# Routing of the first token list: its ranks, its tables and its place in the order, and the weights issued beside it

## The chip, the core and the metric

The kernel runs on one core of a Trainium2 chip. The core has TensorE (matrix products, PE in the profile; its weight loads are PEld), VectorE (DVE), ScalarE (ACT), GpSimd (POOL) and SyncE (SP), and 16 DMA engines that serve the queues of SP, ScalarE and GpSimd together. Each engine runs its own instructions in order and waits on semaphores for the others. The metric is device time in microseconds (us); lower is better. One percent of this kernel is about 1.9 us.

## What is computed

First attention over 4 batches of 8 heads, 768 positions and 64 numbers a head: heads 0, 2 and 6 see all earlier positions, the others only the first 4 and the last 64. Its output, 3072 tokens of 512 numbers, then goes through a mixture of 8 experts with early exit:

```python
scores = np.where(mask[None, :, :, :], scale * np.matmul(q, k.transpose(0, 1, 3, 2)), -1000000000.0)
a = np.exp(scores - np.max(scores, axis=-1, keepdims=True))
a = a / (np.sum(a, axis=-1, keepdims=True) + 1e-09)
x = np.matmul(a, v)                       # and the heads laid side by side: (3072, 512)

do_compute = (x @ w_skip) > 0
out = x.copy()
xc = x[do_compute]
logits = xc @ w_gate
e_idx = np.argmax(logits, axis=1)
gate_w = softmax(logits)[np.arange(len(xc)), e_idx]
for e in range(8):
    m = e_idx == e
    y[m] = gate_w[m, None] * (np.maximum(xc[m] @ w1[e], 0.0) @ w2[e])
out[do_compute] = xc + y
```

Each expert has w1 (512 x 1024) and w2 (1024 x 512) in float32, 33.5 MB for all.

## The kernel before

**Two plans.** The kernel writes its instructions from two planned schedules. A `Plan` holds operations with an engine, an assumed duration, dependences and a key; `lay` walks assumed time and on each engine takes, of the operations that are ready, the one with the lowest key. So the order on each engine comes from the keys (table `K`) and the assumed durations; on the chip only that order and the semaphores remain. The first plan is the attention with the first half of the routing, the second one is the experts. `HOLD` and `X3` are assumptions of the second plan: when each engine is free for it, and when the output of batch 3 has landed. In the built program the framework may place instructions of the second plan ahead of the last ones of the first where they do not depend on them.

**Attention.** It runs over 16 pairs of heads, i = 0 to 15, four to a batch. A pair's q, k and v are loaded (SP), cast to float16 (`Cq`, `Ck`, `Cv`, mostly GpSimd), transposed (TensorE) and copied out of PSUM (`Oq` on ScalarE, `Ok` on VectorE, `Kx` and `Vx` on GpSimd; `Vx` is the copy vx<-va). TensorE forms the scores (`E`, tile pst), ScalarE takes the exponential (`X`, tile at), TensorE weighs the values (`PV`, line 950, tile opsa). v carries along its products with the gate and skip weights (tiles vT and vw, `Ov`, `Vw`, `Ow`), so that the weighing also yields the expert logits. VectorE normalizes: `Nr` (recs, line 969), `Nl` (lgh, line 976) and `Nx` (x, line 986; of pair 15 ScalarE does it, line 1009). Behind each batch `Gs` sums the logits (glog, line 1000), and x of the batch goes to the output tensor (`xo`, line 995; batch 3 in two halves, one from SP and one from ScalarE).

**Routing.** The tokens that compute are sorted into 16 slots' tiles t = 0 to 15 of 128 rows, two for each expert. Even tiles are filled from a first list, made of batches 0 to 2 (18 columns of 128 tokens); odd tiles take the overflow of the first list and the second list, batch 3 (6 columns). `steps` writes one list: VectorE finds the expert of each token (mx, sub, eq, m2, m2x, oh, cnt), TensorE ranks the tokens within each expert (`ranks`, lines 1099 to 1111, tile rk), VectorE and GpSimd make of the rank two sets of tables, L and R (tiles tL and tR: 128 x 384 elements an instruction for the first list, six L and three R), and TensorE multiplies them into the slots' row numbers and gate weights (`slots`, line 1225, tile mps). `fin_a` ("idxA": msb, idx, gsl) turns the first list's into the indices of the even tiles, `fin` ("idx") those of the odd ones.

**Experts.** GpSimd fetches each tile's 128 rows out of the output tensor by indirect DMA (`G`, line 1305, tiles xga and xg). Even tiles need idxA and the output of batches 0 to 2; odd ones need idx and all four batches. VectorE casts (line 1354), TensorE transposes, then w1 (line 1395, tile hps), ScalarE's ReLU (line 1406, tile ht), w2 (line 1417, tile yps), VectorE adds to the row (line 1423), and GpSimd scatters the rows back (line 1315).

**Weights.** w1 and w2 of 8 experts are 16 tiles, n = 0 to 15. Each is fetched in two halves by GpSimd (line 445), which cast to float16 on the way: 512 KB land for each half, from 1 MB of float32. `PARTS` lists the halves issued during the attention, each with the operation of GpSimd behind which it stands; 11 of the 32. The rest is issued between the gathers and scatters: in `GORDER` a number is a gather of that tile, -1 the next half. At most 8 of GpSimd's DMAs are in flight.

Of the kernel before, what the change touches and what calls it, by code (L numbers as in the profile page):

```python
# [15 lines left out]
ACT = mybir.ActivationFunctionType  # L16
# [12 lines left out]
E = 8  # L29
# [25 lines left out]
class Plan:  # L55
# [332 lines left out]
def kernel(  # L388
# [14 lines left out]
    nc = tc.nc  # L403
# [10 lines left out]
    Ov = out.rearrange("(b n p) d -> b p n d", b=B, p=P)  # L414
# [4 lines left out]
    if used % 1024:  # L419
# [14 lines left out]
    def wtile(n, pool):
# [62 lines left out]
    with tc.tile_pool(name="qk", bufs=1) as qk_pool, \  # L497
# [20 lines left out]
        op, dma = pl.op, pl.dma  # L518
# [128 lines left out]
        K = dict(r=229.5, rp=254, Cq=-153.5, Ck=-310.5, Cv=-193, W=-501,
                 Tq=-7.5, Tk=-7, Oq=506.5, Ok=-46, OkA=-661.5, Kx=-754.5,
                 Tv=-1.5, Ov=-26, Vw=-110, Ow=-501, Vx=-131, E=7.5, X=-43,
                 PV=17.5, Nr=154, Nl=72.6, Nx=-91.8, Gs=62.65, sl=-166.5,  # L650
                 z=-122, Wc=-90, xa=-254)
# [32 lines left out]
        for o in order:  # L684
            w, n = o[:2]
# [151 lines left out]
        for i in range(NPR):  # L837
            k0 = 10 * i
# [200 lines left out]
        for n, (name, eng) in enumerate((("SP", nc.sync), ("ACT", nc.scalar))):  # L1039
            m = NQB // 2 * n  # L1040
# [20 lines left out]
        def route(ph, c0, n, fns, pool, psum):  # L1061
# [15 lines left out]
            rl = t("rl", [P, n], FP16)  # L1077
            if ph == 0:
# [3 lines left out]
                olo, ohi = t("olo", [P, n, 8], FP16), t("ohi", [P, n, 16], FP16)  # L1082
# [34 lines left out]
            v = nc.vector  # L1117
            u = v if ph else nc.gpsimd

            def rsel_full():  # L1120
                v.tensor_mul(rsel, rk(), o)
                if ph == 0:
# [26 lines left out]
                                                op=ALU.add),  # L1149
# [12 lines left out]
            if ph == 0:  # L1162
# [3 lines left out]
                    op=ALU.is_ge)  # L1166
# [20 lines left out]
            T[ph, "at"] = table  # L1187

            for m in range(0, n, step):
                e = v if ph else nc.gpsimd  # L1190
                a, b = c0 + m, c0 + m + step
                fns["R", m] = lambda m=m, e=e: e.tensor_tensor(
                    table("R", 0)[:, m:m + step].rearrange(
                        "p c (t v) -> p c t v", v=4),
                    oht[:, m:m + step].unsqueeze(3).to_broadcast(
                        [P, step, nt, 4]),
                    va[:, m:m + step].unsqueeze(2).to_broadcast(
                        [P, step, nt, 4]), op=ALU.mult)
                if ph == 0:
                    for m3 in (m, m + 3):  # L1200
                        fns["L", m3] = lambda m=m3: nc.gpsimd.tensor_tensor(
                            table("L", m)[:, m % 9:m % 9 + 3].rearrange(
                                "p c (h l) -> p c h l", l=8),
                            ohi[:, m:m + 3].unsqueeze(3).to_broadcast(
                                [P, 3, 16, 8]),
                            olo[:, m:m + 3].unsqueeze(2).to_broadcast(
                                [P, 3, 16, 8]), op=ALU.mult)
                    continue
                fns["L", m] = lambda m=m, e=e: e.tensor_tensor(
                    table("L", m)[:, m:m + step],  # L1210
                    iota16.unsqueeze(1).to_broadcast([P, step, P]),
                    rl[:, m:m + step].unsqueeze(2).to_broadcast([P, step, P]),
                    op=ALU.is_equal)
# [17 lines left out]
        def steps(ph, c0, n, k0, last, pool, psum):  # L1231
            f = {}
            route(ph, c0, n, f, pool, psum)
            prev = [last, ("route", 3)]
            w = n * 0.008
            order = ["mx", "sub", "eq", "m2", "m2x", "oh"]
            for nm in order:
                op(("r", ph, nm), "DVE", 0.18 + w, f[nm], prev, k0)
                prev = [("r", ph, nm)]
            op(("r", ph, "ex"), "ACT", 0.25 + w, f["ex"], [("r", ph, "sub")],  # L1240
               -50 if ph else k0 - 30)
            op(("r", ph, "ranks"), "PE", 0.1 * n, f["ranks"],
               [("r", ph, "oh"), ("r", 0, "sums")],
               k0 - 33 if ph == 0 else -50,
               take=None if ph else ("tps", ("r", ph, "rsel")))
            prev = [("r", ph, "oh")]
            on_pool = ("te", "g16", "glo", "rl", "ohi")
            for nm in ["sums", "te", "sm", "gate", "g16", "glo"]:
                op(("r", ph, nm), "POOL" if ph == 0 and nm in on_pool else "DVE",
                   0.17 + w, f[nm],  # L1250
                   prev + ([("r", ph, "ex")] if nm == "sm" else []), k0 + 0.1)
                prev = [("r", ph, nm)]
            prev = [("r", ph, "ranks")]
            if ph:
                op(("r", 1, "oht"), "DVE", 0.2, f["oht"], [("r", 1, "te")],
                   k0 + 0.15)
            for nm in (["rsel", "rank", "rl"] if ph else
                       ["rsel", "rank", "h128", "rl", "tt", "oht", "ge", "hi",
                        "lo", "olo", "ohi"]):
                op(("r", ph, nm), "POOL" if ph == 0 and nm in on_pool else "DVE",  # L1260
                   0.18 + w, f[nm],
                   prev + ([("r", ph, "te")] if nm == "tt" else []),
                   k0 + 0.2)
                prev = [("r", ph, nm)]
            on, ms = ("DVE", [0]) if ph else ("POOL", [0, 6, 12])
            for m in range(0, 1 if ph else n, 3):
                op(("r", ph, "L", m), on, 0.9 if ph else 0.8, f["L", m],
                   [("r", ph, "rl" if ph else "ohi")], K["rp"] if ph == 0 else k0 + 0.3)
            for m in ms:
                op(("r", ph, "R", m), on, 0.6 if ph else 0.9, f["R", m],  # L1270
                   [("r", ph, "oht"), ("r", ph, "glo")],
                   K["rp"] if ph == 0 else k0 + 0.25)
# [57 lines left out]
    with tc.tile_pool(name="moe_w", bufs=1, reuse_waits="tile") as mw_pool, \  # L1330
# [16 lines left out]
        op, dma = pl.op, pl.dma  # L1347
# [148 lines left out]
        for m, t in enumerate(live):  # L1496
            n = of[t][0]
# [6 lines left out]
        for n, (e, ts) in enumerate(jobs):  # L1504
# [94 lines left out]
```

## Time and profile before

| | |
|---|---|
| time, median of 3 runs | 187.7 us (187.51 to 188.92) |
| the profiled execution: its own time / its span | 188.18 us / 186.4 us |
| granted TensorE clock, mean | 0.941 |
| busy share: TensorE / weight loads / VectorE / ScalarE / GpSimd | 79% / 63% / 58% / 55% / 72% |
| chain that ended last, by engine | DMA 51%, PE 14%, POOL 12%, issue 8% |
| DMA time by queue: GpSimd / SP / ScalarE | 54.3% / 38.8% / 2.0% of 16 engines' span |

Times within the profile are counted from the start of the span. The attention ends at about 97 us and the experts follow. The prediction is made against this one execution, which took half a microsecond more than the median. Its page gives this row for the mean share of the DMA engines, in 40 slices of 4.66 us (a digit is a tenth):

```profile
DMA  5999989999999899999999999999999999999520
```

After the load of the first inputs it falls below nine tenths in two slices only, until the last weights are in.

### The profile page before, as it was taken

Reading aid. Unit: us, or ns where it says so; the run is one execution under the profiler, and the core shown is the slowest. Engines: PE = TensorE matmul, PEld = TensorE weight load, DVE = VectorE, ACT = ScalarE, POOL = GpSimd, SP = SyncE. Lnnn points to the kernel's source line nnn. Section 1 sums busy time; section 2 is a strip of 40 time slices with the busy share of each in tenths; the row PEclk is TensorE's granted clock in tenths of the full one; section 3 lists DMA queues with packets and bytes.
Section 4 is the critical chain, followed back from the end, with each engine's and each line's share of the span. In section 5 each row is a group of like instructions: output and inputs, shape, how many; then the busy total and the mean of one; then the engine's idle time right before and its main releaser. Section 6 shows DMA issues by size and latency. Waiting matters only on the chain.

```text
span 186.4 us, 4870 instructions
## 1 busy us (share of the span) xinstructions
PE 148.0 (79%) x1929; PEld 118.3 (63%) x1929; DVE 108.1 (58%) x241; ACT 103.2 (55%) x145; POOL 133.4 (72%) x233
## 2 busy tenths in 40 slices
PE   0689798799999889989933029997997999999900
PEld 0567686698888778878722028876786785757400
DVE  6675567677878748888969523353444355730320
ACT  2575987698998999989629902404203412403000
POOL 7558779999999999997695686356567768525440
PEclk9999999999999999999985558999999999999995
DMA  5999989999999899999999999999999999999520
GB/s 162 315 289 357 342 287 392 390 286 343 276 380 327 274 367 212 203 168 243 252 252 247 353 215 236 213 261 226 262 237 226 183 229 214 200 237 232 148 75 5
DMA packets 27633, 47.12 MB, mean 253 GB/s; under 512 B 5187, under 2 KB 19139, under 8 KB 27603
## 3 DMA queue, kind: packets, MB, share of 16 engines
q0 software_dynamic: 7312, 21.55, 54.3%
q1 hardware_dynamic: 18560, 23.99, 38.8%
q10 hardware_dynamic: 1730, 1.20, 2.0%
q8 instruction: 17, 0.28, 0.6%
q14 instruction: 14, 0.11, 0.2%
HBM read 56.64 MB, written 10.49 MB: 360 GB/s over the span
## 4 chain that ended last, share of the span: by engine, by line
DMA 51%; PE 14%; POOL 12%; issue 8%; SPq 5%; DVE 3%; ACT 2%; POOLq 0%; DVEq 0%
DMA out_dram<-x 13%; DMA w<-in_moe_w_dram 12%; DMA qf<-in_q_dram 9%; DMA xga<-out_dram,idx 7%; DMA out_dram<-xga,idx 6%; DMA xg<-out_dram,idx 5%; PE pst L898 4%; SPq L660 4%; PE opsa L950 3%; PE pst L886 3%; POOL out_dram L1315 3%; PE tps L740 2%; POOL k L712 2%; POOL va L718 1%; POOL q L712 1%
## 5 line engine op out<-in xcount | busy, mean ns | idle before, releaser
L908 ACT ACTIVATE at<-pst 128x1024 f16<-128x1024 f32 (+1 forms) x60 | 58.9, 1013 | 9.7 <-PE pst L898 9.3
L1406 ACT ACTIVATE ht<-hps 128x512 f16<-128x512 f32 x32 | 16.9, 601 | 48.3 <-PE hps L1395 44.2
L898 PE MATMUL pst<-qT,k 128*128 128x128 f16 (+2 forms) x308 | 36.3, 236 | 0.0
L1395 PEld LDWEIGHTS <-w 128*128 128x128 f16 x352 | 31.6, 146 | 4.1 <-issue 1.7
L1395 PE MATMUL hps<-xT,w 128*128 128x128 f16 (+1 forms) x352 | 32.5, 252 | 1.7 <-DVE xT L1379 1.5
L780 DVE COPY k<-tps 64x768 f16<-64x768 f16 x27 | 25.7, 953 | 12.0 <-PE tps L740 11.1
L898 PEld LDWEIGHTS <-k 128*128 128x128 f16 x308 | 24.6, 99 | 10.0 <-issue 3.2
L1417 PE MATMUL yps<-w,ht 128*128 128x512 f16 x128 | 30.4, 379 | 0.0
L886 PE MATMUL pst<-smask,identb 128*128 128x512 bf16 (+2 forms) x64 | 21.6, 348 | 2.3 <-ACT at L908 2.2
L950 PE MATMUL opsa<-va,at 128*128 128x74 f16 x392 | 20.3, 197 | 2.3 <-DVE x L986 2.3
L950 PEld LDWEIGHTS <-at 128*128 128x128 f16 x472 | 18.5, 97 | 2.7 <-DVE x L986 2.5
L445 POOL DMA_DIRECT2D w<-in_moe_w_dram x33 | 18.9, 580 | 1.1 <-PE yps L1417 0.7
L1417 PEld LDWEIGHTS <-ht 128*128 128x128 f16 x128 | 12.0, 98 | 12.1 <-issue 0.5
L1305 POOL DMA_INDIRECT xg<-out_dram,idx x10 | 11.3, 1135 | 9.9 <-ACT ht L1406 4.5
L1315 POOL DMA_INDIRECT out_dram<-xg,idx x10 | 10.1, 1005 | 11.4 <-DMA w<-in_moe_w_dram 4.6
L718 POOL CAST va<-vf 128x768 f16<-128x768 f32 x16 | 13.1, 824 | 1.7 <-DMA vf<-in_v_dram 1.0
L986 DVE TENSOR_TENSOR x<-opsa,recs 128x768 f32<-128x768 f32 x15 | 14.2, 945 | 0.0
L1423 DVE SCALAR_TENSOR_TENSOR xg<-yps,gsl,xg 128x512 f32<-128x512 f32 x10 | 7.4, 747 | 11.4 <-PE yps L1417 11.1
L740 PE MATMUL tps<-ident,q 128*128 128x128 f16 x96 | 8.6, 230 | 6.5 <-DVE q L712 5.9
L766 ACT COPY qT<-tps 128x768 f16<-128x768 f16 x16 | 12.8, 800 | 1.0 <-PE tps L740 0.9
L712 POOL CAST k<-kf 128x768 f16<-128x768 f32 x15 | 12.3, 821 | 1.4 <-PE pst L898 0.8
L1354 DVE CAST x<-xg 128x512 f16<-128x512 f32 x10 | 6.0, 634 | 12.5 <-DMA xg<-out_dram,idx 12.5
(146 smaller groups left out, 252.8 us busy)
## 6 DMA issues: line engine op xcount, KB each, us to landing
w<-in_moe_w_dram POOLq DMA_DIRECT2D x31, 512.0 KB
qf<-in_q_dram SPq DMA_DIRECT2D x16, 384.0 KB, 6.9
kf<-in_k_dram SPq DMA_DIRECT2D x15, 384.0 KB, 6.5
out_dram<-x SPq DMA_DIRECT2D x3, 1536.0 KB, 18.0
out_dram<-x SPq DMA_DIRECT2D x1, 768.0 KB
out_dram<-x ACTq DMA_DIRECT2D x1, 768.0 KB, 8.4
w<-in_moe_w_dram POOLq DMA_DIRECT2D x2, 256.0 KB
kf<-in_k_dram ACTq DMA_DIRECT2D x1, 384.0 KB, 4.5
```

Of the source, the lines that this page charges most:

```text
L445: nc.gpsimd.dma_start(out=wts[e, half][:, c], in_=(w1r, w2r)[half][e][:, c])
L712: e.tensor_copy(t, f)
L718: nc.gpsimd.tensor_copy(vab[i % 3][:, :, GX:GX + 2 * D].rearrange("p n (h d) -> p h n d", h=2), fp32_of("v", i))
L780: nc.vector.tensor_copy(to, ti)
L886: nc.tensor.matmul(pst[:, c0 - c * CH:c0 - c * CH + m].rearrange("p (n c) -> p n c", c=P), identb, mv, start=(n == 0), stop=(n == last))
L898: nc.tensor.matmul(pst[:, c0 - c * CH:c0 - c * CH + m * P], lt, qTs[i][:, qb * P:(qb + m) * P], start=(n == 0), stop=(n == last))
L908: nc.scalar.activation(ats[i][:, c * CH:c * CH + cn], psts[i, c][:, :cn], ACT.Exp, scale=SCALE)
L950: nc.tensor.matmul(opss[i][:, hi, qb * VA:(qb + 1) * VA], ats[i][:, b0 + c:b0 + c + P], vb, start=(n == 0), stop=(n == len(todo) - 1))
L1315: moved(nc.gpsimd.indirect_dma_start(out=out[:n, :], out_offset=bass.IndirectOffsetOnAxis(ap=idx[:, t:t + 1], axis=0), in_=row(t), in_offs ...
L1395: nc.tensor.matmul(hpss[n, b][:, fi, :], w1[:, s, m * b + fi], xTs[n][:, s, :w], start=(fi == 0 and s == 0), stop=(fi == m - 1 and s == DS ...
L1406: nc.scalar.activation(hts[n][:, m * b:m * (b + 1), :w], hpss[n, b], ACT.Relu)
L1417: nc.tensor.matmul(ypss[t], hts[n][:, j, c:c + P], w2[:, j], start=(j == 0), stop=(j == FS - 1))
```

## The change

It edits numbers that set the order, and moves four instructions to another engine. The arithmetic is the same.

- **Ranks.** The first list's `ranks` has a key of its own, `rk` = -44 (before: r - 33 = 196.5), and an assumed duration half as long. A low key lets it stand on TensorE as soon as it is ready.
- **Tables.** Two of the first list's three R (columns 6 and 12) and two of its six L (12 and 15) go from GpSimd to VectorE.
- **The list's keys.** `r`, the key of VectorE's steps of the first list, goes from 229.5 to 93, and the other keys are set anew.
- **Weights.** `PARTS` has 10 halves, not 11: four behind Vx of pair 10 as before, four behind Vx of pair 13 and two behind that of pair 14. Before, four stood behind Cv of pair 14, two behind Vx 13 and one behind Vx 14.
- **The experts' order.** `GORDER` issues gathers 0, 2 and 4 in a row and then three halves; before, a half stood behind each. `HOLD` and `X3` get smaller.

```diff
-    PARTS = [("Vx", 10)] * 4 + [("Cv", 14)] * 4
-    PARTS += [("Vx", 13)] * 2 + [("Vx", 14)]
+    PARTS = [("Vx", 10)] * 4 + [("Vx", 13)] * 4 + [("Vx", 14)] * 2
...
-    GORDER = (0, -1, 2, -1, 4, -1, -1, 1, -1, 3, -1, 5, -1, -1, 6, 7, -1, -1, 8, 9,
+    TAB_DVE = dict(L=(12, 15), R=(6, 12))
+    GORDER = (0, 2, 4, -1, -1, -1, 1, -1, 3, -1, 5, -1, -1, 6, 7, -1, -1, 8, 9,
               -1, -1, 10, 11, -1, -1, 12, 13, -1, -1, 14, 15)
-    HOLD, X3 = dict(POOL=4.5, PE=0.5, DVE=1.0, ACT=4.0), 13.0
+    HOLD, X3 = dict(POOL=0.3, PE=0.0, DVE=0.2, ACT=2.2), 7.5
...
-        K = dict(r=229.5, rp=254, Cq=-153.5, Ck=-310.5, Cv=-193, W=-501,
...
+        K = dict(r=93, rp=245.5, Cq=-155, Ck=-251.5, Cv=-254.5, W=-522,
...
+                 Wc=-90, xa=-254, rk=-44)
...
-                e = v if ph else nc.gpsimd
+                e = v if ph or m in TAB_DVE["R"] else nc.gpsimd
...
-                        fns["L", m3] = lambda m=m3: nc.gpsimd.tensor_tensor(
+                        e3 = v if m3 in TAB_DVE["L"] else nc.gpsimd
+                        fns["L", m3] = lambda m=m3, e=e3: e.tensor_tensor(
...
-            op(("r", ph, "ranks"), "PE", 0.1 * n, f["ranks"],
+            op(("r", ph, "ranks"), "PE", 0.05 * n, f["ranks"],
                [("r", ph, "oh"), ("r", 0, "sums")],
-               k0 - 33 if ph == 0 else -50,
+               K["rk"] if ph == 0 else -50,
...
+                dve = ph or m in TAB_DVE["L"]
+                op(("r", ph, "L", m), "DVE" if dve else "POOL",
+                   0.9 if ph else 0.55 if dve else 0.8, f["L", m],
+                   [("r", ph, "rl" if ph else "ohi")], k0 + 0.3 if dve else K["rp"])
```

What stands where in the built program is seen at three places. The first is GpSimd while pairs 13 and 14 are prepared (w_1_67 and w_1_68 are w1 and w2 of expert 1; vx_143<-va_140 is the copy `Vx` of pair 13). Rows with - stand only before, with + only after:

```order
-L718 CAST va_141<-vf 128x2x6x64
-L787 COPY kx_1_138<-k_1_134 64x4x64
-L788 COPY kx_1_138<-k_1_134 64x4x4
-L445 DMA w_1_67<-in_moe_w_dram 128x2048 x2
-L445 DMA w_1_68<-in_moe_w_dram 128x2048
+L787 COPY kx_1_138<-k_1_134 64x4x64
+L788 COPY kx_1_138<-k_1_134 64x4x4
+L718 CAST va_141<-vf 128x2x6x64
 L823 COPY vx_143<-va_140 64x296
 L825 COPY vx_143<-va_140 64x296
-L445 DMA w_1_68<-in_moe_w_dram 128x2048
```

The three halves ahead of the copy and the one behind it are gone from here; the four follow behind it in two pairs, and one of three halves of expert 2 stands behind the third gather.

The second is TensorE where the first list's product stands (mps<-tR,tL; its first matmul is mps<-c). Before:

```order
L1101 LDWEIGHTS ones_81
L1101 MATMUL rk<-oh,ones_81 128x8
L1106 LDWEIGHTS ones_81
L1106 MATMUL rk<-full,ones_81 128x48
L1222 LDWEIGHTS ones_81
L1222 MATMUL mps<-c_82,ones_81 128x64
L1225 LDWEIGHTS tL_0_2213
L1225 MATMUL mps<-tR_0_2190,tL_0_2213 128x64
```

After, where at is the exponential of pair 14 in the first rows and of pair 15 in the last:

```order
L950 LDWEIGHTS at
L950 MATMUL opsa<-vx_142,at 128x74
L1223 LDWEIGHTS ones_81
L1223 MATMUL mps<-c_82,ones_81 128x64
L1226 LDWEIGHTS tL_0_2209
L1226 MATMUL mps<-tR_0_2178,tL_0_2209 128x64
...
L1226 LDWEIGHTS tL_1_2212
L1226 MATMUL mps<-tR_0_2178,tL_1_2212 128x64
L950 LDWEIGHTS at
L950 MATMUL opsa<-va_139,at 128x74
```

The product stood behind the second list's ranks (rk), which need the logits of batch 3. Now its 19 matmuls stand between the weighing of pair 14 and that of pair 15.

The third is VectorE behind the second list's count (cnt), where msb, idx and gsl are idxA. Before:

```order
L1091 TENSOR_REDUCE cnt<-oh 128x8
L1139 TENSOR_SCALAR r_te<-r_m2x 128x6
L1154 TENSOR_TENSOR r_oht<-iota_86,r_te 128x48
L1121 TENSOR_TENSOR r_rsel<-rk,oh 128x48
L1148 TENSOR_REDUCE r_rank<-r_rsel 128x6
L1158 TENSOR_SCALAR r_rl<-r_rank 128x6
L1209 TENSOR_TENSOR tL_0_2352<-iota_86,r_rl 128x768
L1142 TENSOR_REDUCE r_sm<-r_ex 128x6
L1143 RECIPROCAL r_gate<-r_sm 128x6
L1144 CAST val<-r_gate 128x6
L1145 TENSOR_TENSOR val<-r_gate,val 128x6
L1436 COPY msb<-mps 128x64
```

After:

```order
L1137 SCALAR_TENSOR_TENSOR oh<-r_m2x,r_eq 128x48
L1091 TENSOR_REDUCE cnt<-oh 128x8
L1441 COPY msb<-mps 128x64
L1444 SCALAR_TENSOR_TENSOR idx<-msb 128x8
L1446 TENSOR_TENSOR gsl<-msb 128x8
L1444 SCALAR_TENSOR_TENSOR idx_100<-msb 128x8
L1446 TENSOR_TENSOR gsl_101<-msb 128x8
L1139 TENSOR_SCALAR r_te<-r_m2x 128x6
L1142 TENSOR_REDUCE r_sm<-r_ex 128x6
L1143 RECIPROCAL r_gate<-r_sm 128x6
L1144 CAST val<-r_gate 128x6
```

idxA stood behind ten steps of the second list and now stands right behind cnt. The four tables stand, on VectorE, behind r_olo and ahead of recs, lgh and x of pair 14. On this engine r_rsel, the step that takes up the ranks, now stands ahead of recs, lgh and x of pair 13, and r_olo is behind them as before.

More of the change, by code (lines that the diff above doesn't have):

```diff
@@ L644 @@
         op("mism", "DVE", 1.0, c_mism, ["wgl"], 61)
-        K = dict(r=229.5, rp=254, Cq=-153.5, Ck=-310.5, Cv=-193, W=-501,
[L648 to L651, printed above, removed]
+        K = dict(r=93, rp=245.5, Cq=-155, Ck=-251.5, Cv=-254.5, W=-522,
+                 Tq=-4.5, Tk=-1.5, Oq=564, Ok=-101, OkA=-572, Kx=-820.5, Tv=0,
+                 Ov=-59.5, Vw=-92.5, Ow=-498.5, Vx=-126, E=8.5, X=-90.5, PV=19,
+                 Nr=-5, Nl=64.6, Nx=-218.3, Gs=15.15, sl=-166.5, z=-152.5,
+                 Wc=-90, xa=-254, rk=-44)
         f32 = {}
@@ L1264, in steps @@
                 prev = [("r", ph, nm)]
-            on, ms = ("DVE", [0]) if ph else ("POOL", [0, 6, 12])
+            ms = [0] if ph else [0, 6, 12]
             for m in range(0, 1 if ph else n, 3):
-                op(("r", ph, "L", m), on, 0.9 if ph else 0.8, f["L", m],
-                   [("r", ph, "rl" if ph else "ohi")], K["rp"] if ph == 0 else k0 + 0.3)
+                dve = ph or m in TAB_DVE["L"]
+                op(("r", ph, "L", m), "DVE" if dve else "POOL",
+                   0.9 if ph else 0.55 if dve else 0.8, f["L", m],
+                   [("r", ph, "rl" if ph else "ohi")], k0 + 0.3 if dve else K["rp"])
             for m in ms:
-                op(("r", ph, "R", m), on, 0.6 if ph else 0.9, f["R", m],
+                dve = ph or m in TAB_DVE["R"]
+                op(("r", ph, "R", m), "DVE" if dve else "POOL",
+                   0.6 if ph else 0.55 if dve else 0.9, f["R", m],
                    [("r", ph, "oht"), ("r", ph, "glo")],
-                   K["rp"] if ph == 0 else k0 + 0.25)
+                   k0 + 0.25 if dve else K["rp"])
             if ph:
```

## The prediction, made before the changed kernel had run

> **What bounds the kernel now.** First I read the table by windows. Its columns are the window, its length, the busy time of TensorE, its weight loads, VectorE, ScalarE and GpSimd (number of instructions), the granted TensorE clock, the mean busy share of the 16 DMA engines, and GB/s written.
>
> ```profile
> 72.00:76.00 4.00, 4.00 (x72) 3.49 (x69) 2.70 (x6) 3.69 (x5) 3.75 (x8) 1.00 1.06 217
> 80.00:84.00 4.00, 3.45 (x65) 2.92 (x63) 3.30 (x10) 3.44 (x5) 3.86 (x10) 1.00 0.94 176
> 96.00:100.00 4.00, 0.86 (x20) 0.69 (x16) 2.86 (x8) 2.40 (x13) 4.00 (x6) 0.53 1.07 254
> 100.00:104.00 4.00, 1.41 (x26) 1.26 (x26) 3.66 (x19) 3.64 (x9) 0.19 (x1) 0.50 1.04 296
> 104.00:108.00 4.00, 0.34 (x6) 0.23 (x6) 1.06 (x7) 3.49 (x7) 3.45 (x4) 0.50 1.00 299
> 136.00:140.00 4.00, 4.00 (x34) 3.47 (x32) 1.16 (x3) 0.59 (x2) 2.69 (x4) 1.00 0.95 238
> 168.00:172.00 4.00, 3.77 (x30) 2.90 (x29) 0.00 (x0) 1.29 (x3) 2.51 (x3) 1.00 1.07 230
> 104.00:172.00 68.00, 58.99 (x530) 44.84 (x531) 27.86 (x61) 19.66 (x38) 43.65 (x50) 0.93 1.04 231
> ```
>
> TensorE is almost empty from 93 to 111, but the DMA engines are not: their share is 0.94 or more in every row, even across that hole. The whole second half moves weights. Next the chain of waits and the end of TensorE's timeline (start, duration, what ran, idle time ahead and its cause).
>
> ```profile
> 79.13 23.68 DMA out_dram<-x
> 104.06 0.98 POOL xga L1305
> 158.38 14.23 DMA w<-in_moe_w_dram
> 169.96 1.97 PE L1395 MATMUL hps<-xT,w 128*128 128x256 f16 x16 [0.23 <-DMA w<-in_moe_w_dram]
> 171.76 5.48 PE L1417 MATMUL yps<-w,ht 128*128 128x512 f16 x24
> ```
>
> The last expert's second half of w1, issued at 158.38, is waited for at 169.96; behind it TensorE runs through to the end. So the end is set by when the weight stream reaches that half, and the stream has hardly a pause from 79 on. What counts is how much weight is left behind the first gather, and any pause put into the DMA queue.
>
> **The change, part by part.** (1) One half fewer ahead of the gathers. These are GpSimd's weight issues, the table work and the first gather, and two lines of the page on issue sizes and times to landing.
>
> ```profile
> 78.38 1.58 POOL L445 DMA_DIRECT2D w<-in_moe_w_dram  x3
> 79.94 0.47 POOL L823 COPY vx<-va 64x296 f16<-64x296 f16 x1
> 80.82 0.53 POOL L445 DMA_DIRECT2D w<-in_moe_w_dram  x1
> 82.54 1.05 POOL L445 DMA_DIRECT2D w<-in_moe_w_dram  x2
> 86.47 0.53 POOL L445 DMA_DIRECT2D w<-in_moe_w_dram  x1
> 91.88 1.99 POOL L1192 TENSOR_TENSOR tR<-r_oht,val 128x384 f16<-128x384 f16 x2 [0.48 <-DVE r_oht L1154]
> 94.63 4.77 POOL L1201 TENSOR_TENSOR tL<-r_ohi,r_olo 128x384 f16<-128x384 f16 x6
> 104.04 1.24 POOL L1305 DMA_INDIRECT xga<-out_dram,idx  x1 [3.85 <-DVE gsl L1441]
> 105.28 0.60 POOL L445 DMA_DIRECT2D w<-in_moe_w_dram  x1
> w<-in_moe_w_dram POOLq DMA_DIRECT2D x31, 512.0 KB
> out_dram<-x ACTq DMA_DIRECT2D x1, 768.0 KB, 8.4
> ```
>
> Before, seven halves are issued between 78.38 and 87.0; after, six, in pairs behind the vx copies of pairs 13 and 14, so from about 80.3. In 72:76 only weights move: 512 KB at 217 GB/s is 2.4 us. That half now stands behind the gathers: **+2.4 us** of stream.
>
> (2) The pause that opens. x of batch 2 (1.57 MB, 4.3 us at the 367 GB/s that the next row shows while x of batch 1 goes out) is issued at about 79 with no weights queued.
>
> ```profile
> 64.00:68.00 4.00, 3.63 (x68) 3.14 (x67) 3.08 (x6) 4.00 (x7) 3.81 (x10) 1.00 1.01 367
> ```
>
> It lands well ahead of today's 102.8 (79.13 + 23.68). But the backlog behind 79 shrinks from 7 x 2.4 + 4.3 = 21.1 us to 6 x 2.4 + 4.3 = 18.7 us and starts at about 81 (two us after x's issue, an estimate), so the queue runs dry at 100 to 101. What feeds it next is x of batch 3, then the gathers. When do they come? VectorE and TensorE decide:
>
> ```profile
> 81.23 0.39 DVE L1131 SCALAR_TENSOR_TENSOR r_eq<-r_sub,erev 128x144 f32<-128x144 f32 x1
> 82.33 0.17 DVE L1135 SCALAR_TENSOR_TENSOR r_m2x<-glog,r_m 128x18 f32<-128x18 f32 x1
> 84.24 0.27 DVE L812 CAST va<-vw 128x108 f16<-128x108 f32 x1 [0.80 <-PE vw L805]
> 93.15 0.88 DVE L1174 TENSOR_TENSOR r_olo<-iota,r_lo 128x144 f16<-128x144 f16 x1
> 94.40 0.94 DVE L986 TENSOR_TENSOR x<-opsa,recs 128x768 f32<-128x768 f32 x1
> 98.71 0.75 DVE L1131 SCALAR_TENSOR_TENSOR r_eq<-r_sub,erev 128x48 f32<-128x48 f32 x1
> 99.73 0.47 DVE L1135 SCALAR_TENSOR_TENSOR r_m2x<-glog,r_m 128x6 f32<-128x6 f32 x1
> 100.48 0.25 DVE L1091 TENSOR_REDUCE cnt<-oh 128x8 f16<-128x48 f16 x1
> 101.70 0.96 DVE L1209 TENSOR_TENSOR tL<-iota,r_rl 128x768 f16<-128x768 f16 x1
> 103.33 0.22 DVE L1436 COPY msb<-mps 128x64 f32<-128x64 f32 x1
> 103.92 0.35 DVE L1192 TENSOR_TENSOR tR<-r_oht,val 128x192 f16<-128x192 f16 x1
> 95.40 1.03 PE L950 MATMUL opsa<-va,at 128*128 128x74 f16 x25 [2.34 <-DVE x L986]
> 97.60 2.56 ACT L1009 ACTIVATE x<-opsa,recs 128x64 f32<-128x64 f32 x12 [3.48 <-DVE lgh L976]
> 100.19 0.42 ACTq L995 DMA_DIRECT2D out_dram<-x  x1
> ```
>
> Up to r_olo the change only permutes VectorE's work; its one wait there is the 0.80 at 84.24, and r_olo's 0.88 is long because GpSimd's table ran beside it. With both saved r_olo ends at about 93.0 instead of 94.0. Ranking at once is thus worth at most a microsecond: the ranks came late, but VectorE was full in the meantime.
>
> Then four tables are new on VectorE. Between the 192-element row (0.35) and the 768-element row (0.96), 384 elements take 0.55. Lower bound of four: 2.2 us. Upper bound: each also waits out one GpSimd table (4.77 / 6 = 0.8): 5.4 us. Nearest are r_eq and r_m2x: 0.39 and 0.17 alone, 0.75 and 0.47 beside GpSimd's tables, so 0.3 to 0.36 of waiting each. I take 0.9 a table, 3.6 us: 93.0 to 96.6. GpSimd's four remaining L end at 96.3. Recs, lgh and x of pair 14 follow on VectorE (1.4 us): 98.0. The slots' product now stands ahead of the last pair's weighing on TensorE; it is ready at about 97.2 and so just hidden behind that x; if the tables were later, it would hold the last pair itself. The last pair starts at 98.0 instead of 95.40: +2.6 (bounds: +1.4, +4.5).
>
> That shift carries over to ScalarE's x of batch 3 and its two issues: 102.2 and 102.8 instead of 99.6 and 100.19, so data from about 104.2. Before, the stream passed from x of batch 2 to x of batch 3 at about 101.9 without a pause (1.07 and 1.04 in 96:104). The stream behind it starts **2.3 us later** (+1.1 to +4.2).
>
> (3) The first gather. idxA moves directly behind cnt; that chain also loses 0.7 us of waiting beside tables (r_eq, r_m2x). cnt ends at 100.73 + 2.6 - 0.7 = 102.6 and the gather follows 0.7 later: 103.4 instead of 104.04 (bounds 102.2 and 105.2). What the earlier list gains, the later last pair takes back.
>
> (4) GORDER. Three gathers (1.05 each and 0.3 between) now stand ahead of the first weight issue: 107.4 instead of 105.28. That costs nothing while x of batch 3 (4.3 us) and three gathers fill the engines to about 110; without that cover it would cost up to 2. Gather 1 then waits for x of batch 3, which landed 8.4 us after its issue before: 111.2, with GpSimd there at 109.2 and all later issues queued behind. Three halves (7.2 us) cover that.
>
> (5) The other keys permute the attention of batches 0 to 2: the same instructions, and TensorE and ScalarE stay full in 72:84. I take 0, within 0.5 either way.
>
> (6) Given back: the stream has small pauses today (0.95 in 136:140, 0.94 in 80:84). A longer backlog closes some: 0 to 1.2 us, taken as **-0.6**.
>
> Sum: 2.4 + 2.3 - 0.6 = +4.1 us (ends +2.3 and +6.6). On the profiled execution that is 186.4 + 4.1 = 190.5 us of span (its own time 188.18, half a microsecond over the median); on the median 187.7 + 4.1 = **191.8 us**.
>
> **A rule against the change.** The rows of r_eq and r_m2x show VectorE waiting when both its inputs are in SBUF. The Trainium skill, page "SBUF — State Buffer", section "Who interferes with whom", says that such an instruction and a GpSimd one that reads SBUF exclude each other for the whole instruction. The trace agrees for VectorE; GpSimd's own six tables show no loss (0.8 each). By that rule the eight tables run one after the other.
>
> **Rivals.** Strict turns: 4 x 0.55 + 4 x 0.8 = 5.4 us of tables, last pair at 99.9, gather at 105.2; the upper ends of (2) and (6) make +6, 193.7 us. For it: r_eq, r_m2x and r_olo; against: GpSimd's undisturbed 4.77.
>
> No change: the wait at 169.96 is only 0.23, and TensorE is busy 59 of 68 us from 104 to 172, so it is nearly a bound too. If the pause is the smallest (+1.1), all of 1.2 is recovered, and x and weights that no longer alternate save another us, the delay is about +1: 188.7 us. Against: a stream with share 1.04 has little left to recover.
>
> Faster: the list is what TensorE waits for at 111, and TensorE is the bound behind it. With the gather at 102.2, TensorE starts 1.8 us earlier and the end follows: 185.9 us. It decides if the awaited half lands by 168; today it lands at 169.9 with one half less in front, which speaks against it. That the change does not do what it says is partly so: weights still start a microsecond behind x of batch 2; but the gather waits for idxA, not for that x.
>
> **How the numbers follow.** Forecast 0.47, strict turns 0.18, no change 0.22, faster 0.13. About 1% (1.9 us) is what a measurement of this kernel can tell from no change: slower 0.65, within 0.22, faster 0.13. The range 188.0 to 193.8 leaves out the faster case, the lowest part of no change and the top of strict turns, some 0.2.
>
> **What would show it.** Right: last pair's weighing between 97 and 100; a dip of the DMA share between 99 and 106; first gather within a us or so of 104; x of batch 2 landed before 99; the last weights landing 3 to 5 us later, with longer waits for weights near the end. Wrong: no dip, or the last TensorE block not later though the stream is; or attention ending over a microsecond earlier, which I have priced at nothing.

## The result and the profile after

| | before | changed |
|---|---|---|
| first comparison: median of 4 runs each (range) | 187.6 us (187.44 to 188.92) | 193.34 us (192.08 to 193.87) |
| second comparison (`a_again` below) | 187.38 us (186.27 to 190.28, 7 runs) | 192.46 us (191.54 to 192.94, 4 runs) |
| ratio to before, with its 95% interval | | 1.0305 [1.0248, 1.0361]; 1.0278 [1.022, 1.0335] |
| span of the profiled execution | 186.4 us | 192.2 us |

The changed kernel is slower by 5.7 us (5.1 in the second comparison), 3%; forecast were 4.1 us and a range of 188.0 to 193.8. Medians and ranges here hold every run, ratios leave out the disturbed ones, and where the two disagree it is the ratio that counts.

The table by windows, first two rows of the kernel before that the readings below rest on:

```profile
100.00:112.00 12.00, 3.30 (x46) 2.90 (x47) 5.76 (x26) 7.13 (x15) 7.23 (x10) 0.50 1.03 275
160.00:176.00 16.00, 15.32 (x97) 9.32 (x95) 5.07 (x8) 4.13 (x8) 8.00 (x9) 1.00 0.96 210
```

and of the kernel after:

```profile
96.00:100.00 4.00, 1.37 (x19) 0.93 (x18) 3.97 (x6) 0.00 (x0) 3.48 (x4) 0.72 1.07 215
100.00:104.00 4.00, 2.31 (x36) 2.08 (x34) 1.61 (x6) 0.95 (x5) 0.00 (x0) 0.50 0.35 71
104.00:108.00 4.00, 0.38 (x7) 0.26 (x6) 3.62 (x22) 3.64 (x13) 1.79 (x2) 0.50 0.53 208
160.00:176.00 16.00, 12.34 (x84) 8.10 (x81) 5.46 (x9) 2.06 (x4) 6.80 (x10) 1.00 1.06 234
```

The share of the DMA engines is the number before the last. Where before had 1.04 and 1.00, from 100 to 108, there are 0.35 and 0.53: 4.6 us of DMA time are missing (4 x 0.69 + 4 x 0.47). And near the end, where TensorE was busy for 15.3 of 16 us before, it is busy for 12.3. Its timeline there:

```profile
173.79 1.97 PE L1400 MATMUL hps<-xT,w 128*128 128x256 f16 x16 [0.53 <-DMA w<-in_moe_w_dram]
176.84 1.97 PE L1400 MATMUL hps<-xT,w 128*128 128x256 f16 x16 [1.09 <-DMA w<-in_moe_w_dram]
179.42 3.61 PE L1422 MATMUL yps<-w,ht 128*128 128x512 f16 x16 [0.61 <-DMA w<-in_moe_w_dram]
```

Each of the last blocks now waits for weights, where before had a single wait of 0.23. In the trace, the last packet of weights ends at 175.06 before and at 181.47 after, and the span ends 11.3 and 10.7 later. The time went into the hole behind 100 us. How it came about, by the timelines of VectorE, GpSimd, TensorE, SP and ScalarE, after:

```profile
94.29 0.72 DVE L1174 TENSOR_TENSOR r_olo<-iota,r_lo 128x144 f16<-128x144 f16 x1
94.94 1.65 DVE L1192 TENSOR_TENSOR tR<-r_oht,val 128x384 f16<-128x384 f16 x2
96.51 2.28 DVE L1202 TENSOR_TENSOR tL<-r_ohi,r_olo 128x384 f16<-128x384 f16 x2
99.16 0.94 DVE L986 TENSOR_TENSOR x<-opsa,recs 128x768 f32<-128x768 f32 x1
95.16 4.32 POOL L1202 TENSOR_TENSOR tL<-r_ohi,r_olo 128x384 f16<-128x384 f16 x4 [0.31 <-DVE r_olo L1174]
105.91 1.13 POOL L1310 DMA_INDIRECT xga<-out_dram,idx  x1 [6.43 <-DVE idx L1444]
109.83 1.71 POOL L445 DMA_DIRECT2D w<-in_moe_w_dram  x3
99.54 0.66 PE L1226 MATMUL mps<-tR,tL 128*128 128x64 f16 x9 [0.76 <-POOL tL L1202]
100.16 1.72 PE L950 MATMUL opsa<-va,at 128*128 128x74 f16 x25
113.26 1.86 PE L1400 MATMUL hps<-xT,w 128*128 128x128 f16 x16 [0.58 <-DVE xT L1384]
105.03 0.38 SPq L995 DMA_DIRECT2D out_dram<-x  x1
105.65 0.42 ACTq L995 DMA_DIRECT2D out_dram<-x  x1
```

The tables occupy VectorE until 98.8, so x of pair 14 ends at 100.10; the list's product has its last table at 99.5 and ends at 100.2. Both hold the last pair's weighing, which starts at 100.16 instead of 95.40 and, at a granted clock of 0.50, takes 1.72 instead of 1.03. x of batch 3 is issued at 105.03 instead of 99.58. The ten halves had landed by then (at about 102.6), x of batch 2 too (at 89.4, before at 102.8), so nothing was in the queues. A second execution of the changed kernel (`a_again`) shows the same a microsecond earlier: last pair at 99.01, x of batch 3 issued at 103.88, last weights at 180.55.

### The profile page after: what moved, and what is told of

The parts are those of the page before. It is cut to its first block, busy times and chain, and to the rows that moved or that the text cites. A ratio compares the mean times of both kernels' runs of the same rounds, so it can differ in the third digit from the quotient of the medians.

```text
span 192.2 us, 4852 instructions
## 1 busy us (share of the span) xinstructions
PE 151.4 (79%) x1917; PEld 121.8 (63%) x1929; DVE 109.8 (57%) x245; ACT 103.4 (54%) x145; POOL 131.9 (69%) x229
## 4 chain that ended last, share of the span: by engine, by line
DMA 35%; PE 30%; issue 11%; POOL 7%; DVE 7%; ACT 7%; POOLq 0%; SPq 0%; ACTq 0%; DVEq 0%
DMA w<-in_moe_w_dram 18%; PE pst L898 12%; DMA xg<-out_dram,idx 11%; PE pst L886 5%; PE opsa L950 5%; PE tps L740 4%; ACT at L908 4%; POOL out_dram L1320 3%; DMA vf<-in_v_dram 3%; DMA xga<-out_dram,idx 3%; DVE k L780 3%; PE tps L751 2%; POOL tL L1202 2%; ACT k L778 1%; ACT qT L766 1%
## 5 line engine op out<-in xcount | busy, mean ns | idle before, releaser
L898 PE MATMUL pst<-qT,k 128*128 128x128 f16 (+2 forms) x308 | 37.0, 241 | 0.7 <-ACT at L908 0.7
L1400 PE MATMUL hps<-xT,w 128*128 128x128 f16 (+1 forms) x352 | 33.5, 256 | 3.2 <-DMA w<-in_moe_w_dram 2.6
L1400 PEld LDWEIGHTS <-w 128*128 128x128 f16 x352 | 32.1, 148 | 5.9 <-DMA w<-in_moe_w_dram 3.8
L780 DVE COPY k<-tps 64x768 f16<-64x768 f16 x27 | 25.8, 954 | 12.2 <-PE tps L740 11.3
L898 PEld LDWEIGHTS <-k 128*128 128x128 f16 x308 | 25.2, 101 | 10.4 <-issue 3.8
L950 PE MATMUL opsa<-va,at 128*128 128x74 f16 x392 | 21.2, 201 | 0.0
L950 PEld LDWEIGHTS <-at 128*128 128x128 f16 x472 | 19.4, 101 | 0.2
L886 PE MATMUL pst<-smask,identb 128*128 128x512 bf16 (+3 forms) x52 | 17.8, 354 | 1.6 <-ACT at L908 1.6
L1310 POOL DMA_INDIRECT xga<-out_dram,idx x6 | 7.0, 1174 | 9.4 <-DVE idx L1444 6.4
```

What stands on the lines that cost most here:

```text
L780: nc.vector.tensor_copy(to, ti)
L886: nc.tensor.matmul(pst[:, c0 - c * CH:c0 - c * CH + m].rearrange("p (n c) -> p n c", c=P), identb, mv, start=(n == 0), stop=(n == last))
L898: nc.tensor.matmul(pst[:, c0 - c * CH:c0 - c * CH + m * P], lt, qTs[i][:, qb * P:(qb + m) * P], start=(n == 0), stop=(n == last))
L950: nc.tensor.matmul(opss[i][:, hi, qb * VA:(qb + 1) * VA], ats[i][:, b0 + c:b0 + c + P], vb, start=(n == 0), stop=(n == len(todo) - 1))
L1310: moved(nc.gpsimd.indirect_dma_start(out=row(t), out_offset=None, in_=out[:n, :], in_offset=bass.IndirectOffsetOnAxis(ap=idx[:, t:t + 1], ...
L1400: nc.tensor.matmul(hpss[n, b][:, fi, :], w1[:, s, m * b + fi], xTs[n][:, s, :w], start=(fi == 0 and s == 0), stop=(fi == m - 1 and s == DS ...
```

## The experiments

Each kernel is the changed one (names with a_) or the one before (b_) with the edit shown. The DMA share is that of the window from 100 to 112, where before has 1.03 and the changed kernel 0.63 (0.65 in the second comparison); a share less by 0.1 is 1.2 us of DMA time.

| kernel | median us (runs) | ratio to before [95%] | span | share 100 to 112 |
|---|---|---|---|---|
| `a_half11` | 189.64 (10) | 1.006 [1.0008, 1.0111] | 188.1 | 0.92 |
| `a_half12` | 187.59 (10) | 0.9995 [0.9943, 1.0046] | 185.4 | 1.02 |
| `b_half10` | 190.0 (10) | 1.0055 [0.9997, 1.0113] | 188.0 | 0.82 |
| `b_tab` | 191.88 (4; 189.37 to 193.97) | none | 188.9 | 0.79 |
| `a_again` | 192.46 (4) | 1.0278 [1.022, 1.0335] | 191.2 | 0.65 |
| `a_pool` | 193.35 (4) | 1.0327 [1.0267, 1.0387] | 192.7 | 0.51 |
| `a_late` | 193.62 (4) | 1.0335 [1.0271, 1.04] | 193.1 | 0.46 |
| `a_late_pool` | 190.84 (4) | 1.0228 [1.0166, 1.0289] | 188.3 | 0.78 |
| `a_late_pool_g` | 188.54 (10) | 0.9997 [0.9944, 1.0049] | 186.9 | 0.90 |
| `b_keys` | 186.14 (4) | 0.9883 [0.9807, 0.9959] | 184.8 | 1.06 |
| `a_idx12` | 191.86 (4) | 1.0197 [1.0114, 1.0281] | 189.9 | 1.05 |
| `a_alldve` | 191.69 (1) | none | 190.0 | 0.68 |

The first four were run beside 25 runs of before (median 187.61), the next four beside 7 (187.38), the last four beside 13 (188.28).

### One or two halves more: `a_half11`, `a_half12`

```diff
-    PARTS = [("Vx", 10)] * 4 + [("Vx", 13)] * 4 + [("Vx", 14)] * 2
+    PARTS = [("Vx", 10)] * 4 + [("Vx", 13)] * 4 + [("Vx", 14)] * 3   # * 4 in a_half12
```

The added halves have no duration in the plan, so the order of the attention stays.

> The changed kernel with one more weight half issued behind Vx of pair 14 (11 instead of 10), nothing else moved ahead of the experts. Theory: the 5.7 us lost are DMA time, and most of it is the hole from 101.2 to 106.0 in which the DMA engines have nothing to do; one half is 2.4 us of work that then stands in the hole. So the hole shrinks to about 2.4 us and the time falls by 2.4 us to about 190.9. Rival, TensorE starts its experts late (first product of w1 at 113.26 instead of 111.06) and that sets the end: the time stays at 193.3 within 0.7.

> The changed kernel with two more halves issued behind Vx of pair 14 (12 instead of 10). Theory: the hole of 4.8 us is filled by 2 x 2.4 us, and the time falls by 4.3 to 4.8 us, to 188.5 to 189.0, a microsecond or so above before, which is what the stream lost ahead of 100 us. If TensorE's start, which is still 2.2 us late, shows once the stream is mended, it comes out near 190. Rival, TensorE's start sets the end already: 193.3 within 0.7.

The windows of `a_half12`, and its first product of w1:

```profile
100.00:112.00 12.00, 1.73 (x29) 1.39 (x28) 6.43 (x29) 9.54 (x26) 5.03 (x6) 0.50 1.02 285
```

```profile
113.04 1.86 PE L1400 MATMUL hps<-xT,w 128*128 128x128 f16 x16 [0.58 <-DVE xT L1384]
```

With two halves the hole is gone, and so is the loss: 1.0278 to 0.9995, 2.8% or 5.3 us, though TensorE starts its experts at 113.04, as late as in the changed kernel. TensorE's start is not what it lost by. The 5.3 us are a little more than the 4.3 to 4.8 that were expected. With one half the ratio falls by 2.2%, 4.1 us (by the medians 2.8), more than the 2.4 that were said; part of that is not the half's, since the last pair began at 98.30 there, 0.7 us earlier than in `a_again`. The rival (no gain) falls with both.

### One half fewer, in the kernel before: `b_half10`

```diff
-    PARTS += [("Vx", 13)] * 2 + [("Vx", 14)]
+    PARTS += [("Vx", 13)] * 2
```

> The kernel before with one half fewer (the one behind Vx of pair 14 left to the experts, 10 in all), nothing else moved ahead of the experts. Theory: the weights run out 2.4 us earlier, near 100, x of batch 3 comes no earlier than before, at about 102, so a hole of 2 to 2.4 us opens and the time grows by as much: 189.6 to 190.0. Rival, a half behind the gathers costs nothing since TensorE is the bound from 111 on: 187.6 within 0.7.

The ratio grew by 0.55% (1.0 us, interval 0 to 2.1), the span of the profiled execution by 1.6. The share from 100 to 112 fell from 1.03 to 0.82, 2.5 us of DMA time: the hole is as large as said. By the ratio it cost half of the 2 to 2.4 us that were said; closer than its interval that can't be told.

### The four tables alone, in the kernel before: `b_tab`

```diff
+    TAB_DVE = dict(L=(12, 15), R=(6, 12))
...
-                e = v if ph else nc.gpsimd
+                e = v if ph or m in TAB_DVE["R"] else nc.gpsimd
```

and likewise for L. On VectorE the four stand behind r_olo, on GpSimd they are missing; no other row of the order differs.

> The kernel before with the same four tables of the first list on VectorE behind r_olo, nothing else moved. Theory: in the changed kernel the four took 3.9 us there (94.94 to 98.8), two of them 1.18 us each beside a table of GpSimd; so the last pair's weighing starts at about 99.2 instead of 95.4, x of batch 3 is issued 3.8 us later, a hole of some 3.5 us opens behind 102, and the time grows by 3 to 3.8 us to about 191. Rival, the tables are hidden beside the weight stream: 187.6 within 0.7, with the hole under 1 us.

The last pair's weighing on TensorE:

```profile
99.47 1.72 PE L951 MATMUL opsa<-va,at 128*128 128x74 f16 x25 [5.96 <-DVE x L987]
```

It started at 99.47, after a wait of 5.96 for x of pair 14, where before had 95.40 after 2.34. The share fell to 0.79 (2.9 us). The four executions scatter from 189.37 to 193.97, too widely for a ratio; in the profiled one the last weights land 2.6 us later than before (177.70 against 175.06) and the span is 2.5 us longer, somewhat less than the 3 to 3.8 that were said. Four tables on VectorE are enough to open a hole, and they are not hidden beside the stream.

### What holds the last pair: `a_again`, `a_pool`, `a_late`, `a_late_pool`

```diff
-    TAB_DVE = dict(L=(12, 15), R=(6, 12))
+    TAB_DVE = dict(L=(), R=())                                        # a_pool, a_late_pool
-    HOLD, X3 = dict(POOL=0.3, PE=0.0, DVE=0.2, ACT=2.2), 7.5
+    HOLD, X3 = dict(POOL=4.5, PE=0.5, DVE=1.0, ACT=4.0), 13.0         # a_late, a_late_pool
```

> The changed kernel itself, as the measure for the three others of this call. Both theories: about 3% above before, as when it was first timed (1.0305).

> The changed kernel with all nine tables of the first list on GpSimd; the slots' product still stands ahead of the last pair's weighing. Theory: the last pair is held twice, by the four tables on VectorE ahead of x of pair 14 (100.1) and by the product, which waits for the last table (100.2). Taking the tables off VectorE frees x of pair 14 at about 96.5 but makes nine tables of 0.83 us in a row on GpSimd, the last one done at 101.5 to 102; so the last pair starts at about 102 and the time grows by 1.3 to 1.8 us over the changed kernel. Rival, VectorE's tables alone hold the last pair: it starts near 96.6 and the time falls by about 3.5 us.

> The changed kernel with HOLD and X3 of before, by which the slots' product stands behind the last pair's weighing and idxA behind the second list's steps again; the four tables stay on VectorE. Theory: x of pair 14 still ends at about 100.1, so the last pair starts no earlier, x of batch 3 neither, and the hole stays: within 0.7 us of the changed kernel, though the first gather comes about a microsecond later. Rival, the product alone holds the last pair: it starts about 1.5 us or more earlier and the time falls by as much.

> Both at once: all tables on GpSimd and the product behind the last pair. Theory: nothing holds the last pair any more; it starts at about 96.6, 3.5 us earlier than in the changed kernel, x of batch 3 is issued at 101.5 instead of 105, the hole shrinks from 4.8 to about 1.3 us and the time falls by about 3.5 us to 1% above before, though the first gather is no earlier. Rival, the late gathers and TensorE's late start set the end: no gain over the changed kernel.

The last pair's start on TensorE, first in `a_pool`, where the product of the list (mps) comes ahead of it:

```profile
100.32 0.48 PE L1226 MATMUL mps<-tR,tL 128*128 128x64 f16 x6 [2.02 <-POOL tR L1192]
100.61 1.73 PE L950 MATMUL opsa<-va,at 128*128 128x74 f16 x25
```

in `a_late`:

```profile
99.58 1.72 PE L950 MATMUL opsa<-va,at 128*128 128x74 f16 x25 [5.05 <-DVE x L986]
```

and in `a_late_pool`:

```profile
94.86 1.01 PE L950 MATMUL opsa<-va,at 128*128 128x74 f16 x25 [1.50 <-DVE x L986]
```

`a_again` has this:

```profile
99.01 1.72 PE L950 MATMUL opsa<-va,at 128*128 128x74 f16 x25
```

So either edit alone leaves the last pair where it was or later, once behind the product, once behind x of pair 14; only both together free it, by 4.2 us. That much is as expected, though in `a_pool` it begins 1.4 us sooner than the 102 that was said. The times are not quite. `a_pool` is 0.9 us slower than `a_again`, somewhat less than said. `a_late` is 1.2 us slower, not equal; the ranges of both overlap with that of `a_again`, so neither difference is clear of noise, though the trace of `a_late` shows a cause for its own. GpSimd and the windows of `a_late`:

```profile
108.75 1.13 POOL L1310 DMA_INDIRECT xga<-out_dram,idx  x1 [9.85 <-DVE gsl L1446]
```

```profile
108.00:112.00 4.00, 0.34 (x6) 0.24 (x6) 1.38 (x11) 4.00 (x9) 2.64 (x3) 0.50 0.52 179
```

With idxA behind the second list's steps the first gather came at 108.75, 4 us later than in `a_again`, and the weights stand behind the gathers: the engines were half idle from 108 to 112 as well. And `a_late_pool` won 1.6 us (0.9 by the ratios), not 3.5. GpSimd and the windows of `a_late_pool` show where the rest stayed:

```profile
103.81 1.13 POOL L1310 DMA_INDIRECT xga<-out_dram,idx  x1 [4.23 <-DVE gsl L1446]
107.57 1.80 POOL L445 DMA_DIRECT2D w<-in_moe_w_dram  x3
```

```profile
100.00:104.00 4.00, 1.64 (x32) 1.37 (x31) 3.66 (x19) 4.00 (x8) 0.19 (x1) 0.50 0.99 368
104.00:108.00 4.00, 0.04 (x1) 0.05 (x2) 1.12 (x5) 2.74 (x6) 3.39 (x4) 0.50 0.42 120
```

x of batch 3 now fills 100 to 104, and a new hole opens behind it, since the first weights are issued at 107.57, behind three gathers.

### The order of gathers and weights: `a_late_pool_g`

```diff
-    GORDER = (0, 2, 4, -1, -1, -1, 1, -1, 3, -1, 5, -1, -1, 6, 7, -1, -1, 8, 9,
+    GORDER = (0, -1, 2, -1, 4, -1, -1, 1, -1, 3, -1, 5, -1, -1, 6, 7, -1, -1, 8, 9,
               -1, -1, 10, 11, -1, -1, 12, 13, -1, -1, 14, 15)
```

in `a_late_pool`.

> The last kernel (all tables on GpSimd, the product behind the last pair) with GORDER of before, so that a weight half stands behind each of the first gathers again. There the engines fell idle from 104.2 to 107 behind x of batch 3, until the first weights behind three gathers were issued at 107.6. Theory: with the first half issued behind the first gather, at about 105.3, the hole ends some 2 us sooner and the time falls by 1.5 to 2 us, to 0.5 to 1.5% above before. Rival, the order of gathers and weights costs nothing, as the prediction had it: within 0.7 us of the last kernel, 2.2% above before.

```profile
104.69 0.60 POOL L445 DMA_DIRECT2D w<-in_moe_w_dram  x1
```

In `a_late_pool_g` GpSimd issues the first half at 104.69. The share from 100 to 112 rises from 0.78 to 0.90 (1.4 us), the last weights land 1.4 us sooner (176.21 against 177.60), the median falls by 2.3 us, the ratio by 2.3% (4.3 us; the two ran beside different runs of before). So the new order is not free where nothing covers it: it costs 1.4 us in the profiled executions, and 2.3 or more by the times. In the changed kernel itself x of batch 3 is so late that it covers the three gathers (share 1.00 from 108 to 112).

### The keys and the early ranks alone: `b_keys`

In the kernel before, the table K of the changed kernel, `rk` and the shorter assumed duration of `ranks`.

```diff
-        K = dict(r=229.5, rp=254, Cq=-153.5, Ck=-310.5, Cv=-193, W=-501,
+        K = dict(r=93, rp=245.5, Cq=-155, Ck=-251.5, Cv=-254.5, W=-522,
...
-               k0 - 33 if ph == 0 else -50,
+               K["rk"] if ph == 0 else -50,
```

> The kernel before with the changed keys and the ranks of the first list counted at once, and nothing else: tables on GpSimd, 11 halves, GORDER, HOLD and X3 as before. Theory: VectorE is full until r_olo in any case, so r_olo ends where it did (93 to 95), the last pair and x of batch 3 come as before, no hole opens and the time is that of before within 1%. Rival, the new keys themselves cost about 1 us of DMA time in the attention (the profile of the changed kernel had lost that much ahead of 100 us): 0.5 to 1% slower.

The windows of `b_keys`:

```profile
80.00:100.00 20.00, 13.45 (x248) 11.63 (x247) 17.03 (x47) 14.62 (x28) 16.92 (x33) 0.95 1.06 245
100.00:112.00 12.00, 2.69 (x36) 2.29 (x34) 4.88 (x22) 6.39 (x13) 7.15 (x9) 0.50 1.06 287
```

No hole opened, and the time fell, by 1.2% (0.4 to 1.9%), a little past the 1% that was allowed for; the rival, keys that cost something, falls. r_olo starts at 92.19 against 93.15 before, x of batch 3 is issued at 98.47 against 99.58, the first gather at 103.46 against 104.04, and the share is 1.06 in both windows where before has 1.03, which makes 1.0 us over the 32 us. The last weights land 1.5 us sooner (173.59 against 175.06). Whether the ranks or the other keys did it was not separated. It is the one kernel here that beats both; it differs from `a_late_pool_g` in the main by one half of weights and by where the halves stand (four behind Cv of pair 14, not Vx of pair 13), together worth 1.1% (2.1 us) between them.

### An early list with a full stream: `a_idx12`

`a_half12`, with the list's product and `idxA` as operations of the first plan:

```diff
+        op(("r", 0, "slots"), "PE", 0.9, slots(0, 0, 18, (tr_psum, "tps")),
+           [*(("r", 0, "L", m) for m in range(0, 18, 3)),
+            *(("r", 0, "R", m) for m in (0, 6, 12))], -100, take=("tps", "idxA"))
...
+        op("idxA", "DVE", 0.8, fin_a, [("r", 0, "slots")], -1000)
```

> The changed kernel with 12 halves, and idxA ahead of the last pair's recs on VectorE (product and idxA belong to the first plan): the first gather is issued near 101 instead of 105, TensorE's first product of w1 comes near 109 instead of 113. Theory: with 12 halves the weight stream has no hole, and the time is where the last weights land plus the 10.7 to 11.4 us that have followed them in every run; an earlier first gather moves no weights, so the time stays that of before within 1%. Rival, with the stream mended TensorE's start sets the end: the time falls by 2 us or more, to 1% or more below before.

GpSimd and the windows of `a_idx12`:

```profile
99.34 1.13 POOL L1326 DMA_INDIRECT xga<-out_dram,idx  x1 [1.44 <-DVE gsl L1296]
103.12 1.72 POOL L445 DMA_DIRECT2D w<-in_moe_w_dram  x3
120.30 1.08 POOL L1326 DMA_INDIRECT xga<-out_dram,idx  x1 [15.47 <-DMA out_dram<-x]
```

```profile
116.00:120.00 4.00, 4.00 (x48) 3.09 (x47) 0.75 (x1) 1.23 (x3) 0.00 (x0) 1.00 0.67 178
120.00:124.00 4.00, 1.41 (x14) 0.68 (x12) 0.61 (x1) 0.94 (x2) 3.28 (x4) 1.00 0.39 46
```

The list was early, as meant: first gather at 99.34, first product of w1 at 109.71. Both theories failed on the time, which came out 2% above before (1.1 to 2.8%). The early gathers let three halves go at 103.1, ahead of x of batch 3 at about 104.8. x and weights then alternated, and x landed at about 119. The gather of tile 1 waits for it, until 120.30, with all further weights behind it: the hole came 15 us later, 3.8 us of it (4 x 0.33 + 4 x 0.61).

### All nine tables on VectorE: `a_alldve`

```diff
-    TAB_DVE = dict(L=(12, 15), R=(6, 12))
+    TAB_DVE = dict(L=(0, 3, 6, 9, 12, 15), R=(0, 6, 12))
```

> The changed kernel with all nine tables of the first list on VectorE, GpSimd idle beside them. Theory: a table takes 0.55 us on VectorE when no table of GpSimd runs beside it, nine take about 5 us, and x of pair 14 follows near 100 to 101. Rival, a table takes 1.18 us on VectorE in any case: nine take 10.6 us, and x of pair 14 comes near 106.

The instructions of the L line, first in the changed kernel, then in `a_alldve` (durations in ns: shortest, median, longest):

```profile
L1202 POOL TENSOR_TENSOR tL<-r_ohi,r_olo x4: 1012/1140/1142, 95.2 to 98.3; 128x384 f16<-128x384 f16 x4
L1202 DVE TENSOR_TENSOR tL<-r_ohi,r_olo x2: 1179/1179/1179, 96.5 to 97.6; 128x384 f16<-128x384 f16 x2
```

```profile
L1202 DVE TENSOR_TENSOR tL<-r_ohi,r_olo x6: 552/554/555, 93.7 to 96.0; 128x384 f16<-128x384 f16 x6
```

A table takes 0.55 us on VectorE with GpSimd idle and 1.18 beside one of GpSimd's, which takes 1.14 itself, against 0.83 in the kernel before. The rival (1.18 in any case) falls. x of pair 14 ended at 97.9, earlier than either theory said: the nine took 4.2 us, and r_olo ended at 92.4. From the start of r_olo to the last pair it is 5.9 us in both kernels: nine tables on VectorE take no longer than four there and four on GpSimd.

## Why the prediction was right, and what it had wrong

**The bound: right.** In all 14 profiles the span ends 10.7 to 11.4 us behind the last packet of weights, though that packet lies anywhere from 173.6 to 182.4. Filling the hole (`a_half12`) gave the whole loss back with TensorE still late. One reading under it was off: the prediction took the half awaited at 169.96 for the one issued at 158.38, but its own row has that one land at 172.61 (158.38 + 14.23). In the trace the awaited half is the one issued before it, at 157.84; the argument does not change.

**One half fewer, +2.4: right in kind, its size known roughly.** 2.1 us between `a_late_pool_g` and `b_keys`, 2.7 each for two in `a_half12` (5.3 / 2, but 4.1 for the first and 1.2 for the second), 1.0 (0 to 2.1) in `b_half10`.

**The pause, +2.3: right in its cause, too small.** The stream behind it was to start at 104.2, 2.3 us later than the 101.9 of before. The first packets of x of batch 3 moved at 105.95, in `a_again` at 104.78, so the pause was 4.1 or 2.9 us. With the half's 2.4 that makes 6.5 and 5.3, and the last weights landed 6.4 and 5.5 us later, where 3 to 5 had been said.

It was worked out from a last pair at 98.0; it began at 100.16 (99.01 in `a_again`), and x of batch 3 went out at 105.03 (103.88) instead of 102.2. Half of this or more is r_olo, which was to end at 93.0 and ended at 95.0 (93.9 in `a_again`; over the kernels with the new keys it lies between 92.4 and 95.0). One term was missing: the weighing ran at half the clock, 0.7 us longer. The tables themselves were priced well, 3.85 us against 3.6 for the four on VectorE, and from the end of r_olo to the last pair it took 5.1 us in both executions against the 5.0 forecast. GpSimd's four, priced at an undisturbed 0.8, took 1.14, so the product, which the prediction had just hidden, was as late as x. Against all this, x of batch 3 moved 0.9 us after its issue, not two.

The rival "strict turns", with a last pair at 99.9 and 193.7 us, came nearest to the first comparison, but by luck: it has 6.9 us from the end of r_olo to the last pair. Its rule does not hold as it stands: for one table on each engine it gives 0.55 + 0.83 = 1.38 us, and the pairs came every 1.1. The Trainium skill, page "SBUF — State Buffer", section "Who interferes with whom", says that only the shared pair of ports causes contention, and that it is an exclusive lock. That the two slow each other the trace confirms, but the waits here are 0.63 on VectorE and 0.31 on GpSimd, neither of them a whole table of the other engine. Two sums beside it are slightly off: by the prediction's own terms the bounds of the last pair are +1.2 and +4.4, not +1.4 and +4.5, and the rival's +6 takes term (6) at its middle, not at an end.

**The first gather at 103.4: wrong.** It came at 105.91 (104.76 in `a_again`), since idxA stands behind the last pair's logits, and these were late too. With an x of batch 3 just as late it cost nothing here.

**GORDER at nothing: right here, by the cover named** (share 1.00 from 108 to 112). Without it, 1.4 us in the traces of `a_late_pool` and `a_late_pool_g` and 2.3 or more by their times, where "up to 2" was said.

**The other keys, 0 within 0.5: open.** `b_keys` shows 2.2 us of gain (0.8 to 3.6 by its interval), but for keys and early ranks together, and the ranks had their price in (2), at most a microsecond: r_olo ended at 93.08, as said, instead of 94.03, and x of batch 3 went out 1.1 us sooner. The other microsecond is less than the interval's half-width of 1.4 us, so it is not shown that the other keys gain anything.

**Given back, -0.6: not shown.** The span grew by 0.6 less than the landing of the last weights was delayed (5.8 against 6.4), but since 10.7 us follow it instead of 11.3, which the prediction did not name and no run explains. The share from 112 to 172, where pauses were to close, is 1.04 before and 1.05 after, too near to tell.

In ratios to before: keys and ranks -1.2%, the missing half +1.1%, and tables, product, GORDER and the smaller HOLD and X3 together +2.8 to +3.1% (from 0.9997 to 1.0278 or 1.0305). The last of these compares kernels that ran beside different runs of before, so the split is rough. The bound and the hole were right; that the sum came out as near as it did, 4.1 against 5.1 to 5.7, is partly luck, since what new keys and early ranks gain offsets a pause that was priced too low.

**TensorE's start as the bound ("faster"): against it** stand `a_half12`, 2 us later than before and no slower, and `a_idx12`, 1.4 us earlier and slower.

## What to carry to other kernels

When the DMA engines are the bound, ask of each change which moment they have nothing queued, and what must happen for the next transfer to be issued; work moved onto the engine that prepares that transfer can cost its full length there, though the engine has idle time elsewhere (`b_tab`: the last pair came 4.1 us later for four tables). Splitting a set of instructions between VectorE and GpSimd is worth measuring against leaving all of them on one: here eight split took as long as nine on VectorE. An edit that brings work forward also brings forward the transfers behind it, and these may collide with one that others wait for.

## What was not expected of the hardware

Two engines that work on such tables side by side slow each other: 0.55 to 1.18 us on VectorE, 0.83 to 1.14 on GpSimd. TensorE's granted clock is 0.72 on the mean from 96 to 100, where its work thins out, and 0.50 from 100 on, and the same 25 matmuls took 1.72 us in the changed kernel and 1.01 in `a_late_pool`, where they came 5 us earlier (the clock is 1.00 there from 92 to 98): here the lateness of a short step grew by another 0.7 us. In `a_idx12` three weight halves were issued 1.7 us ahead of x of batch 3 (103.12 against 104.77), and x landed 14.7 us after its issue. On the same queue of ScalarE it took 7.9 us in `a_half12`, which has as many halves ahead of the gathers, and 5.2 in the changed kernel, where the queues were empty.
